# A spectral block and a gMLP on one core: Gelus, a third product's w, and w_in's later tiles put at other chunks

## The chip, the core and the metric

The kernel runs on one core of a Trainium2 chip. The metric is the device time of one execution in microseconds, and the time of a kernel is the median of its runs. The core's engines run side by side: TensorE (PE) multiplies matrices, VectorE (DVE) and ScalarE (ACT) work elementwise, GpSimd (POOL) and SyncE (SP) mostly issue transfers here. Each takes its instructions strictly in the order of the program.

## The reference

Two sublayers stand one after the other, both modulated by a condition `c`:

```python
h = layernorm(x) * (1 + ca) + sa
x = x + ga * (Cr @ (h @ Hr.T) - Ci @ (h @ Hi.T))      # 2048 x 2048 and 512 x 512 DFT matrices
h = layernorm(x) * (1 + cb) + sb
z = gelu(h @ w_in)                                    # 512 -> 1792
z1, z2 = z[..., :896], layernorm(z[..., 896:])
x = x + gb * ((z1 * (w_sp @ z2 + b_sp)) @ w_out)      # w_sp 2048 x 2048, w_out 896 -> 512
```

`x` is 2048 x 512, all in fp32. sa, ca, ga, sb, cb, gb are six rows of `silu(c) @ w_mod`.

## The kernel before, in words

Every fp32 operand is split into a rounded part and a rest (`ah` and `al` for the streamed side, `wh`/`wl`, `w`, `wih`/`wil` and others for the weights), and each product is three matmuls: rounded by rounded, rounded by rest, rest by rounded (`matmul3`, lines 95 to 97). ACT writes the rounded part (line 249 for `ah`), DVE the rest (line 256 for `al`).

The program is one long list of chunks n. Up to N2 they are the DFT over the sequence, from N2 to N3 the first half of `z` (z1), from N3 to N4 the second half (z2), after N4 the product with `w_sp`, and last `w_out`. The order on each engine is written out by hand: `at(n, f, ...)` puts a piece of work at chunk n, and `run(n)` issues what was put there, ahead of the chunk's matmuls in the z1 stage; `prep(n)` ahead of that issues `al` for chunk n + 2 and `ah` for chunk n + 3.

The change lies in the z1 stage. It computes z1 for the four row blocks in two pairs (q = 0, 1), each by seven products (a Strassen-like scheme, `FORMS = (1, 2, 6, 7, 4, 5, 3)`) of two chunks each. So c = n - N2 counts 0 to 27, the first pair is c = 0 to 13, the second c = 14 to 27. Chunks of products 1, 2, 6 and 4 have four column tiles f (12 matmuls), those of 7, 5 and 3 have three (9 matmuls). In the first pair c = 6, 7 is product 7, c = 8, 9 product 4, c = 10, 11 product 5, c = 12, 13 product 3; in the second pair 14 later. Several products add up in the same PSUM banks, so between them somebody has to read a sum out before TensorE goes on:

- After product 7, ACT copies the three banks of `z1g` to `z1k` (line 669); product 4 then goes on in these banks.
- After product 5, DVE adds `z1k` to the three banks of `z1p` (line 677); product 3 then goes on in them. ACT applies the Gelu to the sum later (line 679).
- After products 2 and 4, `gelu_z1` (lines 682 to 686) applies the Gelu to four banks (line 685), each into a tile `z` of the pool tag `z1row`, and POOL stores each tile to DRAM (`z_d`, line 686). That tag has seven buffers, used in turn. For product 2 of the first pair the Gelus were put three chunks after the product, that is at c = 6.

```python
z = zrow[0].tile([P, Q], F32, tag="z1row", bufs=NF, name=f"z1_{q}_{p}_{f}")
nc.scalar.activation(z, acc[f], AF.Gelu_apprx_tanh)
nc.gpsimd.dma_start(z1_d[2 * q + (p == 4)][f], z)
```

Around that stand other pieces: `hi_w(3)` and `lo_w(3)` split the weights of product 3 (line 641 on ACT, line 644 on DVE); `turn_z` transposes blocks of h on DVE (line 597); `load` (line 154) and `load_wi` (line 565) issue loads on SP, `stage<-h_d` being blocks of h; `make_wi` (line 575, ACT) and `make_wi_lo` (line 578, DVE) split the four tiles of w_in's second half (`wih`, `wil`) for the z2 stage; `sum_s` (lines 728 to 739) forms sums of blocks of `w_sp` on DVE and stores them by POOL. The tags `wil2` and `wil3` are also the buffers of product 7's weights.

Of the kernel before, what the change touches and what calls it, by code (L numbers as in the profile page):

```python
# [9 lines left out]
F32R = mybir.dt.float32r  # L10
# [3 lines left out]
P = 128  # L14
# [5 lines left out]
def fnet_gmlp_kernel(  # L20
# [35 lines left out]
    FH = F2 // 2  # L56
# [22 lines left out]
    def bank(k, name):  # L79
        return psum.tile([P, 512], F32, tag=f"bank{k}", bufs=1, name=name)  # L80
# [12 lines left out]
    def matmul3(acc, ah, al, bh, bl, first, last, go_on=False):  # L93

        nc.tensor.matmul(acc, ah, bh, start=first, stop=False, skip_group_check=go_on)  # L95
        nc.tensor.matmul(acc, ah, bl, start=False, stop=False, skip_group_check=go_on)  # L96
        nc.tensor.matmul(acc, al, bh, start=False, stop=last, skip_group_check=go_on)  # L97
# [25 lines left out]
    def at(n, f, *a):  # L123
        fill.setdefault(n, []).append((f, a))

    def run(n):
        for f, a in fill.pop(n, []):
            f(*a)
# [55 lines left out]
    def prep(n):  # L184

        if n not in prepared:
            prepared.add(n)
            if later_hi(n + 2):
                prep_hi(n + 2)
            prep_lo(n + 2)  # L190
            if n % 2 == 0 and n and not N2 + 4 <= n + 4 < N3:
                turn_two(n + 4)
            if n and not later_hi(n + 3):
                prep_hi(n + 3)
# [362 lines left out]
    wi_hi, wi_lo, wraw, ZT = {}, {}, {}, {}  # L557
# [12 lines left out]
    def make_wi(e, k):  # L570
        if k == 0:
            wi_hi[e] = wpool[0].tile([P, ND, FH], F32R, tag="wih", bufs=1, name="wih1")
        wi_hi[e, k] = wi_hi[e][:, k, :]
        wi_lo[e, k] = wpool[0].tile([P, FH], F32R, tag=f"wil{k}", bufs=1, name=f"wil{e}_{k}")
        nc.scalar.activation(wi_hi[e, k], wraw[e, k], AF.Copy)

    def make_wi_lo(e, k):
        nc.vector.tensor_tensor(wi_lo[e, k], wraw.pop((e, k)), wi_hi[e, k].bitcast(F32), op=ALU.subtract)

    WR, WF, ZG = {}, {}, {}  # L580
# [65 lines left out]
    def mm_z1(n):  # L646
        q, c = divmod(n - N2, NP)
        p, k = FORMS[c // 2], c % 2
        nf = 4 if p in (1, 2, 6, 4) else 3
        here, there = (0, 4) if q == 0 else (4, 0)  # L650
        if k == 0 and p in (1, 5):
            for f in range(nf):
                ZT[f] = bank(here + f, f"z1p{q}_{p}_{f}")
        acc = ZG if p in (6, 7, 4) else ZT
        th, tl = AH.pop(n), AL.pop(n)
        for f in range(nf):
            w, cols = WF[1 if f == 3 else p] if p == 6 else WF[p], slice(f * P, (f + 1) * P)
            matmul3(acc[f], w[0][:, k, cols], w[1][:, k, cols], th, tl,
                    k == 0 and p in (1, 5), k == 1, p not in (1, 5))
        if k == 0:  # L660
            return
        if p == 1:
            for f in range(4):
                ZG[f] = bank(there + f, f"z1g{q}_{f}")
                nc.scalar.activation(ZG[f], ZT[f], AF.Copy)
        elif p in (6, 7):
            for f in range(3):
                G[p, f] = bpool[0].tile([P, Q], F32, tag="bh" if p == 6 else "bl", bufs=3, name=f"z1k{q}_{p}_{f}")
                nc.scalar.activation(G[p, f], ZG[f], AF.Copy)
        elif (q, p) == (0, 2):  # L670
            at(n + 3, gelu_z1, q, p, dict(acc))
        elif p in (2, 4):
            gelu_z1(q, p, acc)
        else:
            m = 7 if p == 5 else 6
            for f in range(3):
                nc.vector.tensor_tensor(G[m, f], ZT[f], G[m, f], op=ALU.add)
            for f in range(3):
                nc.scalar.activation(G[m, f], G[m, f], AF.Gelu_apprx_tanh)
                nc.gpsimd.dma_start(z1_d[2 * q + (p == 5)][4 + f], G.pop((m, f)))  # L680

    def gelu_z1(q, p, acc):
        for f in range(4):
# [3 lines that stand above are left out]
# [261 lines left out]
    for s, n in ((4, 4), (5, 4), (6, 6), (7, 6), (8, 10), (9, 10)):  # L948
        m = n + (s == 9)
# [23 lines left out]
    for j, turn, weigh, row, fold, hi in ((0, (25, 26, 27, 28), (29, 29, 30, 30), 26, (34, 34, 35, 36), (38, 35, 36, 37)),  # L973
# [8 lines left out]
        n = weigh[3] + (3 if j == 0 else 1)  # L982
# [13 lines left out]
    for t in range(NQ):  # L996
        n = 8 * NQ * (t + 1)
# [35 lines left out]
    wpool, zpool, zrow, bpool, spre, gpool = [], [], [], [], [], []  # L1033
# [12 lines left out]
    at(84, change_q)  # L1046
    for i, u in enumerate((r, g, b) for g in range(2) for b in range(4) for r in range(2)):
        n = 85 + 5 * i if i < 8 else N2 + (13, 15, 28, 29, 31, 33, 35, 37)[i - 8]
        m = n + (4 if i < 8 or i > 9 else (8, 11)[i - 8])
        at(n, load_s, *u)  # L1050
        at(m, sum_s, *u, True)
        at(m + 1, sum_s, *u, False)
# [7 lines left out]
    for c, *todo in ((2, (norm_y, 3, 2), (hi_w, 6), (lo_w, 6), (sum_w, 7)),  # L1060
                     (3, (norm_y, 3, 3), (sum_w, 4), (post_h, 3, 2), (hi_w, 7), (lo_w, 7)),
                     (4, (hi_w, 4), (lo_w, 4), (post_h, 3, 3), (change_s,), (load, N2 // 4 + 3)),
                     (6, (sum_z4, 0), (hi_w, 5), (lo_w, 5)), (8, (turn_z, 2), (hi_w, 3)), (9, (lo_w, 3), (load_wi, 1, 0)),
                     (10, (load_wi, 1, 2)), (12, (turn_z, 3)), (14, (sum_z, 1)),
                     (17, (make_wi, 1, 0), (make_wi_lo, 1, 0)), (18, (make_wi, 1, 1), (make_wi_lo, 1, 1)),
                     (19, (sum_z4, 1)), (22, (make_wi, 1, 2), (make_wi_lo, 1, 2)), (24, (make_wi, 1, 3), (make_wi_lo, 1, 3))):
        for f, *a in todo:
            at(N2 + c, f, *a)
    for n in range(N2, N3):
        prep(n)  # L1070
        run(n)
        mm_z1(n)

    zstack = ctx.enter_context(ExitStack())

# [5 lines left out]
    for i, p in enumerate(PROD):  # L1081
        for k in range(8):
            n = NB[p] + 2 * k
# [39 lines left out]
    for f in range(NF):  # L1123
        n = NB[6] + 3 * f
# [66 lines left out]
```

## Time and profile before

| | |
|---|---|
| median of 3 runs | 949.35 us (948.96 to 949.91) |
| profiled execution, its own time | 948.98 us |
| its span, first to last instruction | 947.2 us |
| TensorE busy | 940.0 us (99%) |
| VectorE / ScalarE / GpSimd busy | 704.0 / 388.4 / 174.3 us |
| granted clock of TensorE | 1.0 in every slice |

A busy time is the union of an engine's instructions. In a timeline, "0.33 <-ACT z1k" behind an instruction says that its engine stood idle 0.33 us before it, and what ended that. A matmul's shown length (0.39 us) is longer than the step to the next one, since matmuls overlap.

### The profile page before, as it was taken

The numbers are of one execution on the slowest core, as the hardware profiler recorded it, in microseconds if no ns is written. First come the engines' busy times: TensorE is split into PE (matmuls) and PEld (weight loads), VectorE is DVE, ScalarE is ACT, GpSimd is POOL, SyncE is SP. The second block draws the span as 40 slices with busy tenths as digits, with TensorE's granted clock in tenths as the row PEclk, the third lists the DMA queues.
The fourth block names the chain that finished last, engine by engine and source line by source line (L and its number), as shares of the span: only waits on it lengthen the run. The fifth ranks groups of instructions, "written<-read, shape, count | busy, mean of one in ns | idle before, by whom it ended". The sixth has DMA issues, their size and how long they took to land.

```text
span 947.2 us, 12274 instructions
## 1 busy us (share of the span) xinstructions
PE 940.0 (99%) x4160; PEld 781.3 (82%) x4160; DVE 704.0 (74%) x1039; ACT 388.4 (41%) x665; POOL 174.3 (18%) x331
## 2 busy tenths in 40 slices
PE   8999999999999999999999999999999999999998
PEld 5888888888888888888888999888888888888886
DVE  6799857775576667767978588877788688885872
ACT  4685424232132222322776356644544444331221
POOL 2430000221531144122332265200000000000000
PEclk9999999999999999999999999999999999999999
DMA  9996553576437975996397985555554456833541
GB/s 213 222 222 149 113 139 89 147 187 156 134 89 195 274 212 153 279 280 140 126 307 281 327 266 152 155 114 134 128 133 90 105 118 140 206 102 120 192 162 57
DMA packets 249230, 161.25 MB, mean 170 GB/s; under 512 B 130192, under 2 KB 218512, under 8 KB 249040
## 3 DMA queue, kind: packets, MB, share of 16 engines
q1 hardware_dynamic: 235792, 120.75, 52.8%
q0 software_dynamic: 11984, 39.07, 11.3%
q10 hardware_dynamic: 1392, 0.66, 0.3%
q8 instruction: 32, 0.52, 0.2%
q14 instruction: 30, 0.25, 0.1%
HBM read 123.73 MB, written 36.70 MB: 169 GB/s over the span
## 4 chain that ended last, share of the span: by engine, by line
PE 95%; DMA 2%; DVE 1%; ACT 1%; POOL 1%; issue 0%; ACTq 0%; SPq 0%; POOLq 0%; DVEq 0%
PE gp L95 12%; PE gp L96 12%; PE gp L97 12%; PE gw L96 10%; PE gw L97 10%; PE gw L95 10%; PE yp L96 3%; PE yp L95 3%; PE yp L97 3%; PE z2p L97 3%; PE z2p L96 3%; PE z2p L95 3%; PE op L96 3%; PE op L95 3%; PE op L97 3%; PE z1p L95 1%
## 5 line engine op out<-in xcount | busy, mean ns | idle before, releaser
L249 ACT ACTIVATE ah<-t 128x512 fp32r<-128x512 f32 x263 | 164.2, 627 | 306.6 <-PE gp L97 184.9
L256 DVE TENSOR_TENSOR al<-t,ah 128x512 fp32r<-128x512 f32 x264 | 180.1, 685 | 142.7 <-PE gp L96 65.3
L95 PE MATMUL gp<-ah,hh 128*128 128x512 f32 x496 | 192.9, 389 | 0.0
L96 PE MATMUL gp<-al,hh 128*128 128x512 f32 x496 | 192.9, 389 | 0.0
L97 PE MATMUL gp<-ah,hl 128*128 128x512 f32 x496 | 192.9, 389 | 0.0
L97 PE MATMUL gw<-ah,bl 128*128 128x512 f32 x400 | 155.6, 389 | 0.0
L96 PE MATMUL gw<-al,bh 128*128 128x512 f32 x400 | 155.6, 389 | 0.0
L95 PE MATMUL gw<-ah,bh 128*128 128x512 f32 x400 | 155.6, 389 | 0.0
L97 PEld LDWEIGHTS gp<-ah,hl 128*128 128x128 f32 x496 | 93.1, 188 | 19.4
L95 PEld LDWEIGHTS gp<-ah,hh 128*128 128x128 f32 x496 | 93.1, 188 | 19.3
L96 PEld LDWEIGHTS gp<-al,hh 128*128 128x128 f32 x496 | 93.1, 188 | 19.2
L95 PEld LDWEIGHTS gw<-ah,bh 128*128 128x128 f32 x400 | 75.1, 188 | 15.7
L97 PEld LDWEIGHTS gw<-ah,bl 128*128 128x128 f32 x400 | 75.1, 188 | 15.5
L96 PEld LDWEIGHTS gw<-al,bh 128*128 128x128 f32 x400 | 75.1, 188 | 15.5
L220 DVE STREAM_TRANSPOSE t<-stage 128x1024 f32<-128x1024 f32 x64 | 79.2, 1238 | 5.8 <-DMA stage<-in_A_dft_seq_re_dram 5.4
L214 DVE STREAM_TRANSPOSE t<-stage 128x1024 f32<-128x1024 f32 x56 | 69.3, 1238 | 0.0
L761 ACT ACTIVATE bh<-z 128x512 fp32r<-128x512 f32 (+1 forms) x56 | 32.8, 587 | 65.8 <-PE gw L96 65.8
L739 POOL DMA_DIRECT2D s_d<-sj x64 | 35.1, 550 | 110.5 <-DVE sj L731 81.5
L95 PE MATMUL yp<-hth,gh 128*128 128x512 f32 x128 | 49.8, 389 | 0.0
L96 PE MATMUL yp<-htl,gh 128*128 128x512 f32 x128 | 49.8, 389 | 0.0
L97 PE MATMUL yp<-hth,gl 128*128 128x512 f32 x128 | 49.8, 389 | 0.0
L96 PE MATMUL z2p<-wil,ah 128*128 128x448 f32 x128 | 46.7, 365 | 0.0
(204 smaller groups left out, 1419.3 us busy)
## 6 DMA issues: line engine op xcount, KB each, us to landing
stage<-in_A_dft_seq_im_dram SPq DMA_DIRECT2D x64, 256.0 KB, 5.5
sj<-in_B_w_sp_dram SPq DMA_DIRECT2D x32, 512.0 KB, 8.3
s_d<-sj POOLq DMA_DIRECT2D x64, 256.0 KB, 4.3
stage<-s_d SPq DMA_DIRECT2D x128, 128.0 KB, 2.9
stage<-in_A_dft_seq_re_dram SPq DMA_DIRECT2D x60, 256.0 KB, 5.3
stage<-in_B_w_sp_dram SPq DMA_DIRECT2D x96, 128.0 KB, 3.2
stage<-h_d SPq DMA_DIRECT2D x32, 256.0 KB, 6.0
wm<-in_w_mod_dram SPq DMA_DIRECT2D x16, 256.0 KB, 4.8
```

Source lines behind the costliest of these rows:

```text
L95: nc.tensor.matmul(acc, ah, bh, start=first, stop=False, skip_group_check=go_on)
L96: nc.tensor.matmul(acc, ah, bl, start=False, stop=False, skip_group_check=go_on)
L97: nc.tensor.matmul(acc, al, bh, start=False, stop=last, skip_group_check=go_on)
L214: nc.vector.transpose(t.rearrange("p r (b i) -> p r b i", i=32), st[:, :, :, 16 * k:16 * k + 32])
L220: nc.vector.transpose(t.rearrange("p k (b i) -> p k b i", i=32), st[:, :, 32 * k:32 * k + 64].rearrange("p b (k i) -> p k b i", k=2))
L249: nc.scalar.activation(AH[n], source(n), AF.Copy)
L256: nc.vector.tensor_tensor(AL[n], source(n), AH[n].bitcast(F32), op=ALU.subtract)
L739: nc.gpsimd.dma_start(s_d[m, r, g][b * P:(b + 1) * P, :], a)
L761: nc.scalar.activation(BH[p, k][:, :w], b_of(p, k), AF.Copy)
```

## The change

The Gelus of product 2 in the first pair are put five chunks after the product in place of three (c = 8 in place of 6). `hi_w(3)` goes from c = 8 and `lo_w(3)` from c = 9 to c = 10. The ACT parts of w_in's third and fourth tile go from c = 22 to 20 and from c = 24 to 22; the DVE part of the third goes from c = 22 to 21.5, which is run behind the matmuls of c = 21, and that of the fourth stays at 24. The tile `wil` is now taken in `make_wi_lo` and no longer in `make_wi`. The sums of one `w_sp` block (i = 8) go from c = 21 and 22 to c = 22 and 23.

```diff
@@ -571,10 +571,10 @@
         wi_hi[e, k] = wi_hi[e][:, k, :]
+        nc.scalar.activation(wi_hi[e, k], wraw[e, k], AF.Copy)
+
+    def make_wi_lo(e, k):
         wi_lo[e, k] = wpool[0].tile([P, FH], F32R, tag=f"wil{k}", bufs=1, name=f"wil{e}_{k}")
-        nc.scalar.activation(wi_hi[e, k], wraw[e, k], AF.Copy)
-
-    def make_wi_lo(e, k):
         nc.vector.tensor_tensor(wi_lo[e, k], wraw.pop((e, k)), wi_hi[e, k].bitcast(F32), op=ALU.subtract)
@@ -668,7 +668,7 @@
         elif (q, p) == (0, 2):
-            at(n + 3, gelu_z1, q, p, dict(acc))
+            at(n + 5, gelu_z1, q, p, dict(acc))
@@ -1046,7 +1046,7 @@
-        m = n + (4 if i < 8 or i > 9 else (8, 11)[i - 8])
+        m = n + (4 if i < 8 or i > 9 else (9, 11)[i - 8])
@@ -1060,16 +1060,18 @@
-                     (6, (sum_z4, 0), (hi_w, 5), (lo_w, 5)), (8, (turn_z, 2), (hi_w, 3)), (9, (lo_w, 3), (load_wi, 1, 0)),
-                     (10, (load_wi, 1, 2)), (12, (turn_z, 3)), (14, (sum_z, 1)),
+                     (6, (sum_z4, 0), (hi_w, 5), (lo_w, 5)), (8, (turn_z, 2)), (9, (load_wi, 1, 0)),
+                     (10, (hi_w, 3), (lo_w, 3), (load_wi, 1, 2)), (12, (turn_z, 3)), (14, (sum_z, 1)),
-                     (19, (sum_z4, 1)), (22, (make_wi, 1, 2), (make_wi_lo, 1, 2)), (24, (make_wi, 1, 3), (make_wi_lo, 1, 3))):
+                     (19, (sum_z4, 1)), (20, (make_wi, 1, 2)), (21.5, (make_wi_lo, 1, 2)), (22, (make_wi, 1, 3)),
+                     (24, (make_wi_lo, 1, 3))):
     for n in range(N2, N3):
         prep(n)
         run(n)
         mm_z1(n)
+        run(n + 0.5)
```

How this moves the instructions, at three places. First ACT in the first pair, before, from product 5's weights to the copies of product 7 (`w_4178` is product 5's rounded w, `z_0_2_*` product 2's Gelus, `ah_4205` the rounded part for c = 10):

```order
L641 ACTIVATE w_4178<-wraw_0_3923 128x768
L685 ACTIVATE z_0_2_0_4182<-z1p_1_0_4020 128x512
L685 ACTIVATE z_0_2_1_4185<-z1p_1_1_4021 128x512
L685 ACTIVATE z_0_2_2_4188<-z1p_1_2_4022 128x512
L685 ACTIVATE z_0_2_3_4191<-z1p_1_3_4023 128x512
L249 ACTIVATE ah_4205<-hs_3979 128x512 [waits DVE_49,PE_49,Activation_49]
L669 ACTIVATE z1k_7_0_4216<-z1g_0_4048 128x512 [waits DVE_49,PE_49]
L669 ACTIVATE z1k_7_1_4218<-z1g_1_4050 128x512 [waits PE_49]
L669 ACTIVATE z1k_7_2_4220<-z1g_2_4052 128x512 [waits PE_49]
```

And ACT now, from behind product 7's copies (which directly follow `w_4178` and the `ah` for c = 10) to product 3's weights (`z_0_4_*` are product 4's Gelus, `w_4283` product 3's rounded w):

```order
L249 ACTIVATE ah_4212<-hs_3979 128x512 [waits DVE_49,Activation_49]
L685 ACTIVATE z_0_2_0_4222<-z1p_1_0_4020 128x512
L685 ACTIVATE z_0_2_1_4225<-z1p_1_1_4021 128x512
L685 ACTIVATE z_0_2_2_4228<-z1p_1_2_4022 128x512
L685 ACTIVATE z_0_2_3_4231<-z1p_1_3_4023 128x512
L249 ACTIVATE ah_4248<-t_3762 128x512 [waits DVE_49,PE_49,Activation_49]
L685 ACTIVATE z_0_4_0_4267<-z1g_0_4048 128x512 [waits PE_49]
L685 ACTIVATE z_0_4_1_4270<-z1g_1_4050 128x512 [waits PE_49]
L685 ACTIVATE z_0_4_2_4273<-z1g_2_4052 128x512 [waits PE_49]
L685 ACTIVATE z_0_4_3_4276<-z1g_3_4054 128x512 [waits DMASW4_49,PE_49,Activation_49]
L249 ACTIVATE ah_4281<-t_3762 128x512 [waits DVE_49]
L641 ACTIVATE w_4283<-wraw_2_3928 128x768
```

Product 2's Gelus now stand behind the copies and directly ahead of product 4's; product 3's w stood ahead of product 4's Gelus and stands behind them. The wait on DMASW4 in `z_0_4_3` is for the store of `z_0_2_0`, whose buffer it takes, the eighth tile of seven buffers. It stood there before too.

Second, DVE in the first pair, where `w_4284` (`w_4235` before) is the rest of product 3's w, `al_4304` that for c = 13, and line 677 the sums in product 5's banks:

```order
-L644 TENSOR_TENSOR w_4235<-wraw_2_3928,w_4234 128x768 [waits Activation_49]
-L256 TENSOR_TENSOR al_4283<-t_3762,ah_4251 128x512 [waits DVE_49,PE_49,Activation_49]
-L256 TENSOR_TENSOR al_4304<-t_3762,ah_4285 128x512 [waits DVE_49,PE_49,Activation_49]
-L677 TENSOR_TENSOR z1k_7_0_4216<-z1p_5_0_4292,z1k_7_0_4216 128x512 [waits PE_49]
```

```order
+L256 TENSOR_TENSOR al_4279<-t_3762,ah_4248 128x512 [waits DVE_49,PE_49,Activation_49]
+L644 TENSOR_TENSOR w_4284<-wraw_2_3928,w_4283 128x768 [waits Activation_49]
+L256 TENSOR_TENSOR al_4304<-t_3762,ah_4281 128x512 [waits DVE_49,PE_49]
+L677 TENSOR_TENSOR z1k_7_0_4204<-z1p_5_0_4292,z1k_7_0_4204 128x512 [waits PE_49]
```

The rest of w went from two places ahead of `al_4304` to one, so it is the last but one ahead of the sums of line 677.

Third, DVE in the second pair now (`wil_2` and `wil_3` are the rests of w_in's third and fourth tile, `sj` the w_sp block's sums, `al_4622` the rest for c = 27):

```order
L578 TENSOR_TENSOR wil_2_4546<-wraw_2_4287,wih_4443 128x896
L256 TENSOR_TENSOR al_4548<-hs_4376,ah_4529 128x512
L731 TENSOR_TENSOR sj_4351<-sj_4351 128x512
L732 TENSOR_TENSOR sj_4351<-sj_4351 128x512
L256 TENSOR_TENSOR al_4569<-hs_4376,ah_4550 128x512
L735 TENSOR_TENSOR sj_4351<-sj_4351 128x512
L736 TENSOR_TENSOR sj_4351<-sj_4351 128x512
L256 TENSOR_TENSOR al_4601<-hz_4214,ah_4571 128x512
L217 STREAM_TRANSPOSE t_4603<-stage_4217 128x4x4x32 x2
L578 TENSOR_TENSOR wil_3_4608<-wraw_2_4287,wih_4443 128x896
L256 TENSOR_TENSOR al_4622<-hz_4214,ah_4606 128x512
L677 TENSOR_TENSOR z1k_7_0_4540<-z1p_5_0_4610,z1k_7_0_4540 128x512
```

`wil_2` stood behind the four sums of `sj` and stands ahead of them, each of the two pairs of sums with one `al` more ahead of it; `wil_3` keeps its place, but its ACT half now comes two chunks earlier.

## Rows read from the trace of the kernel before

**Rows 1.** The page, busy time, share and count by engine.
```profile
PE 940.0 (99%) x4160; PEld 781.3 (82%) x4160; DVE 704.0 (74%) x1039; ACT 388.4 (41%) x665; POOL 174.3 (18%) x331
```
**Rows 2.** Waits of PE, whole run, without the start's: total us, times, longest.
```profile
...
PE z1p L95 <- DVE z1k L677: 0.4, 1, 0.4
...
PE z1g L95 <- ACT z1k L669: 0.3, 1, 0.3
```
**Rows 3.** Timeline of PE, start us and us, first pair (c = 8, c = 12).
```profile
468.41 0.39 PE L97 MATMUL z1g<-ah,w 128*128 128x512 f32 x1
469.13 0.50 PE L95 MATMUL z1g<-ah,wh 128*128 128x512 f32 x1 [0.33 <-ACT z1k L669]
469.46 0.40 PE L96 MATMUL z1g<-al,wh 128*128 128x512 f32 x1
...
478.78 0.39 PE L95 MATMUL z1p<-ah,w 128*128 128x512 f32 x1
```
**Rows 4.** Timeline of PE, second pair, the start of c = 26.
```profile
512.55 0.39 PE L97 MATMUL z1p<-ah,w 128*128 128x512 f32 x1
513.33 0.47 PE L95 MATMUL z1p<-ah,w 128*128 128x512 f32 x1 [0.39 <-DVE z1k L677]
```
**Rows 5.** Timeline of ACT, first pair.
```profile
465.30 0.83 ACT L641 ACTIVATE w<-wraw 128x768 fp32r<-128x768 f32 x1
466.03 2.04 ACT L685 ACTIVATE z<-z1p 128x512 f32<-128x512 f32 x4
467.94 0.65 ACT L249 ACTIVATE ah<-hs 128x512 fp32r<-128x512 f32 x1
468.46 1.59 ACT L669 ACTIVATE z1k<-z1g 128x512 f32<-128x512 f32 x3
...
472.86 2.69 ACT L685 ACTIVATE z<-z1g 128x512 f32<-128x512 f32 x4
```
**Rows 6.** Timeline of ACT, second pair, copies of product 7.
```profile
501.47 0.63 ACT L249 ACTIVATE ah<-hs 128x512 fp32r<-128x512 f32 x1 [1.46 <-PE z1g L97]
502.10 1.96 ACT L669 ACTIVATE z1k<-z1g 128x512 f32<-128x512 f32 x3
```
**Rows 7.** Timeline of DVE, first pair.
```profile
468.14 0.95 DVE L644 TENSOR_TENSOR w<-wraw,w 128x768 fp32r<-128x768 f32 x1
469.01 0.68 DVE L256 TENSOR_TENSOR al<-hz,ah 128x512 fp32r<-128x512 f32 x1
469.61 0.68 DVE L256 TENSOR_TENSOR al<-hs,ah 128x512 fp32r<-128x512 f32 x1
...
477.62 2.05 DVE L677 TENSOR_TENSOR z1k<-z1p,z1k 128x512 f32<-128x512 f32 x3 [0.16 <-PE z1p L97]
```
**Rows 8.** Timeline of DVE, second pair.
```profile
503.83 0.69 DVE L731 TENSOR_TENSOR sj<-sj 128x512 f32<-128x512 f32 x1 [1.89 <-DMA sj<-in_B_w_sp_dram]
...
508.74 0.69 DVE L256 TENSOR_TENSOR al<-hz,ah 128x512 fp32r<-128x512 f32 x1
...
510.89 1.10 DVE L578 TENSOR_TENSOR wil<-wraw,wih 128x896 fp32r<-128x896 f32 x1 [0.24 <-ACT wih L575]
...
512.50 1.88 DVE L677 TENSOR_TENSOR z1k<-z1p,z1k 128x512 f32<-128x512 f32 x3
```
**Rows 9.** Timelines of SP and of POOL, first pair: issues of transfers.
```profile
468.64 6.93 SPq L154 DMA_DIRECT2D stage<-h_d  x8
...
473.75 0.54 POOL L686 DMA_DIRECT2D z_d<-z  x1 [4.71 <-ACT z L685]
```
**Rows 10.** DMA issues of four stretches (466.9, 468.5, 473.75, 475.84 us): us to landing.
```profile
z_d<-z POOLq DMA_DIRECT2D x1, 256.0 KB, 2.4
...
z_d<-z POOLq DMA_DIRECT2D x1, 256.0 KB, 4.6
...
z_d<-z POOLq DMA_DIRECT2D x1, 256.0 KB, 6.0
...
z_d<-z POOLq DMA_DIRECT2D x1, 256.0 KB, 6.8
```

More of the change, by code (lines that the diff above doesn't have):

```diff
@@ L573, in make_wi @@
         wi_hi[e, k] = wi_hi[e][:, k, :]
-        wi_lo[e, k] = wpool[0].tile([P, FH], F32R, tag=f"wil{k}", bufs=1, name=f"wil{e}_{k}")
         nc.scalar.activation(wi_hi[e, k], wraw[e, k], AF.Copy)
     def make_wi_lo(e, k):
+        wi_lo[e, k] = wpool[0].tile([P, FH], F32R, tag=f"wil{k}", bufs=1, name=f"wil{e}_{k}")
         nc.vector.tensor_tensor(wi_lo[e, k], wraw.pop((e, k)), wi_hi[e, k].bitcast(F32), op=ALU.subtract)
```

## The prediction

> **What bounds the kernel now.** I read the page first: TensorE is busy for 940.0 of 947.2 us [rows 1]. So a change of order can only give back TensorE's idle time, or add to it. Next came TensorE's waits over the whole run. Behind the program's start, which the change doesn't touch, there are just two, both in the z1 stage [rows 2]. The timeline of TensorE prices them. Undisturbed, matmuls start 0.227 us apart: from 469.46 to 478.78 there are 41 steps [rows 3]. At c = 8 the step is 0.72 and the next one 0.33 in place of 0.23, which makes 0.60 us lost to the copies of product 7 [rows 3]. At c = 26 the step is 0.78; with the same slow second step 0.65 us are lost, to the sums of line 677 [rows 4]. Both together are 1.25 us, 0.13% of the time. What a measurement of this kernel can tell from no change is about 0.2%, 1.9 us. So the change can't be measurably faster; the question is whether it makes a new wait.
>
> **The Gelus of product 2, c = 6 to 8.** Before, ACT runs w, the four Gelus (2.04 us), `ah` and only then the copies, which start at 468.46 [rows 5], though the first bank is complete when its last matmul is, before 467.5 (its tile is the first of three in c = 7, whose last matmul starts at 468.41 [rows 3]). In the second pair, where no Gelus stand ahead, `ah` and copies run directly after each other from 501.47 [rows 6], and TensorE has no wait there [rows 2]. So the first wait goes: **-0.60 us**, and TensorE would start c = 12 at 478.78 - 0.60 = 478.18.
>
> The Gelus themselves, 2.0 us, move into a stretch of ACT that was half idle, and nobody on TensorE waits for them before c = 10. But what hangs on their stores does wait. The buffer of the first Gelu tile is taken again by the last Gelu of product 4 once the store has landed. Before, this store is issued at 466.90 with nothing else under way and lands in 2.4 us [rows 10], long before the last Gelu of product 4 (its four end at 475.55 [rows 5]). Now: the last copy starts after the last matmul of c = 7 (468.41 + 0.39, and 0.1), takes 0.65 (1.96 for three [rows 6]) and ends at 469.5; `ah` follows, and 0.52 later [rows 5], at 469.9, the first Gelu. A store is issued 0.89 us after its Gelu starts (472.86 and 473.75 [rows 5, 9]): at 470.8. By then SP has been issuing eight loads of 256 KB since 468.64 [rows 9]; these wait for the stores of h, not for any Gelu, so they don't move. A store that meets these loads lands after 4.6 us (issued at 468.5, as they begin) to 6.8 (475.84, at their end); one issued in their midst at 473.75 needs 6.0 [rows 10]. Lower bound 2.4, the lone store, upper bound 6.8. I take 5.3, midway between 4.6 and 6.0, since at 470.8 about half of the loads are ahead of it. It then lands at 476.1, and the last Gelu of product 4, which could have run to 475.55 - 0.60 = 474.95, runs from 476.2 to about 476.8 (0.6 each, four in 2.04 to 2.69 [rows 5]).
>
> **Product 3's w, c = 8 and 9 to 10.** It stands behind that Gelu now. Counted from the Gelu's end E: `ah` starts at E - 0.13 and w 0.52 later (466.03 + 2.04 against 467.94, then 468.46 [rows 5]); w takes 0.83 [rows 5]; the rest of w on DVE 0.87 and an `al` 0.60 to the next start [rows 7]; then the first sum of line 677, and 0.83 after its start TensorE (512.50 and 513.33 [rows 8, 4]). That is E + 3.5 with some hundredths between engines, call it 3.55. Before, these sums waited for TensorE alone: 0.16 idle at 477.62 [rows 7]. With E = 474.95, were there no store, TensorE would start c = 12 at 478.50 instead of 478.18, 0.42 lost with the slow second step. With E = 476.8 it starts at 480.35: 2.17 and 0.1, **+2.27 us**. The load of w_in's second half waits for the rest of w on SP, and so issues later; it is first read at c = 20, ten chunks on (some 23 us at 9 to 12 steps each), and costs nothing.
>
> **w_in's third and fourth tile, and the sums a chunk later.** ACT's part at c = 20 fits into the 1.46 us for which ACT was idle ahead of 501.47 [rows 6]. `wil_2` writes a buffer of product 7's weights, so it can't start before c = 21 ends. That is 42 matmuls before 512.78 (512.55 + 0.23 [rows 4]), at 503.2, just when DVE sat idle for 1.89 us until 503.83 [rows 8]. From 503.4 it takes 1.1, the four sums 0.7 each, two `al` 0.6 each: done by 508.5, still ahead of the `al` at 508.74 that follows TensorE [rows 8]. `wil_3` no longer waits 0.24 us for ACT [rows 8], and the sums of line 677, two instructions behind it, start that much earlier: **-0.24 us** of the second wait. Nothing on this path depends on the first pair's delay, since both follow TensorE. The stores of the sums go a chunk later through POOL, ahead of the Gelus' stores as before; nothing reads them before the `w_sp` stage, cost 0.
>
> **Sum:** -0.60 + 2.27 - 0.24 = +1.43 us on the profiled 948.98, 950.4. The median of the runs lies 0.37 higher, 949.35, so I forecast **950.8 us**, +0.15%, too little to be told from no change. With the landing at 4.6 to 5.8 us it is 950.1 to 951.3.
>
> **Rivals.**
> 1. *The store lands later*, the side of slower. Place: the last Gelu of product 4. Each us of landing time is a us on TensorE; from 5.8 us on the whole passes +1.9. At the 6.8 us of the last store in the stretch the sum is 1.43 + 1.5 = 2.93: 952.3. For it: all stores later in the stretch took 6.0 and more [rows 10]. Against: those had SP's next loads (w_in) around them, and more loads ahead.
> 2. *The store is not in the way*: it lands within 3.4 us of its issue. Then -0.60 + 0.42 - 0.24 = -0.42: 948.9. For it: a lone store takes 2.4, and this one is not issued last. Against: the store at 468.5, with only the first loads near it, took 4.6 already [rows 10]. The Trainium skill, "DMA: Bandwidth & Descriptors", section "Queues, rings and completion order", says that each DMA engine takes turns between the queues that have work, packet by packet; by that the store would share with one load at a time and not stand behind several. The trace speaks against it, with 6.0 us for 256 KB at 473.75 as against 2.4 alone.
> 3. *Both old waits go altogether and none comes*: -1.25, 948.1. It needs the rest of w to be done before the sums' banks are complete, which the chain above denies by 0.3 us.
> 4. *w_in's move does nothing*: if `wil_2` pushes the `al` at 508.74 back by more than the 0.24 us won, the second wait stays: 951.0, inside the forecast's range.
>
> **How the numbers follow.** Forecast with rival 4: 0.61. Rival 1: 0.23. Rival 2: 0.13. Rival 3: 0.03. Faster by over 0.2% would need more than all idle time there is: 0.02 for what I don't see. Slower by over 0.2%: 0.24, nearly all rival 1. Same: 0.74. The forecast's own range is 950.1 to 951.3; to hold 8 in 10 it must reach to 952.3, rival 1's time, and down to 949.0, which takes in some of rival 2 with the scatter of the runs (0.4 us below the median).
>
> **What would show it.** In the changed profile TensorE's wait for the copies at c = 8 is gone, and c = 8 starts at about 468.6. The store of the first Gelu is issued near 470.8 and lands near 476; ACT stands idle, released by that store, ahead of the last Gelu of product 4; TensorE waits about 2.2 us for line 677 at c = 12; at c = 26 its wait shrinks from 0.39 to about 0.15. I am wrong if ACT has no idle time ahead of that Gelu (rival 2), if the store takes over 5.8 us (rival 1), if the copies still hold c = 8, or if the granted clock drops from 1.0 behind the wait, which no row here shows for a pause of that length.

## The result, and the profile after

| | before | after |
|---|---|---|
| median | 949.11 us (948.80 to 949.91, 18 runs) | 950.51 us (949.72 to 952.68, 18 runs) |
| profiled execution, its span | 948.98, 947.2 us | 952.28, 950.5 us |
| mean granted clock of the profiled execution | 1.0 | 0.998 |

The ratio is 1.0018, with a 95% interval of 1.001 to 1.0025; by the medians the change costs 1.40 us, 0.15%. That is less than the 0.2% that the prediction took for the least that can be told from no change, but the interval lies above 1: 18 runs against 18 do tell it. The forecast was 950.8 us, in a range of 949.0 to 952.3, and the working made the difference +1.43 us. Of the 18 runs, 14 lie between 949.72 and 950.71 (median 950.45) and four between 952.18 and 952.68, all four at a mean granted clock of 0.998. The profiled execution is one of these four; what they have in addition is the last part of this section.

TensorE is still the bound [rows 1]. Its count of matmuls is the same; the 1.8 us that it is busy longer come of the slower matmuls shown below:

```profile
PE 941.8 (99%) x4160; PEld 782.7 (82%) x4160; DVE 703.7 (74%) x1039; ACT 388.5 (41%) x665; POOL 174.5 (18%) x331
```

In TensorE's waits the row of the copies [rows 2] is gone, and that of line 677 is five times as long (and belongs to another place, c = 12 and no longer c = 26):

```profile
PE z1p L95 <- DVE z1k L677: 2.2, 1, 2.2
```

TensorE's timeline says where. The last column in brackets is the idle time before an instruction and what ended it.

```profile
468.65 0.39 PE L97 MATMUL z1g<-ah,w 128*128 128x512 f32 x1
468.87 0.39 PE L95 MATMUL z1g<-ah,wh 128*128 128x512 f32 x1
...
474.09 0.39 PE L97 MATMUL z1g<-ah,wl 128*128 128x512 f32 x1
...
478.17 0.39 PE L97 MATMUL z1p<-ah,w 128*128 128x512 f32 x1
480.73 0.47 PE L95 MATMUL z1p<-ah,w 128*128 128x512 f32 x1 [2.17 <-DVE z1k L677]
481.03 0.40 PE L96 MATMUL z1p<-al,w 128*128 128x512 f32 x1
...
481.73 0.62 PE L96 MATMUL z1p<-al,w 128*128 128x512 f32 x1
...
485.14 0.40 PE L95 MATMUL z1p<-ah,w 128*128 128x512 f32 x1
...
516.23 0.39 PE L97 MATMUL z1p<-ah,w 128*128 128x512 f32 x1
516.65 0.47 PE L95 MATMUL z1p<-ah,w 128*128 128x512 f32 x1
```

At c = 8 the step from 468.65 to 468.87 is the undisturbed one: the wait for the copies [rows 3] is gone. At c = 12 the step is 2.56 us, and the next 0.30: 2.41 us are lost. At c = 26 the step is 0.42 us where it was 0.78 [rows 4].

ACT shows what c = 12 hangs on: product 2's Gelus and three of product 4's, then 2.10 us of nothing, then the fourth, and behind it `ah` and product 3's w.

```profile
470.09 2.05 ACT L685 ACTIVATE z<-z1p 128x512 f32<-128x512 f32 x4
472.00 0.66 ACT L249 ACTIVATE ah<-t 128x512 fp32r<-128x512 f32 x1
472.52 1.92 ACT L685 ACTIVATE z<-z1g 128x512 f32<-128x512 f32 x3
476.54 0.60 ACT L685 ACTIVATE z<-z1g 128x512 f32<-128x512 f32 x1 [2.10 <-PE z1p L97]
477.03 0.62 ACT L249 ACTIVATE ah<-t 128x512 fp32r<-128x512 f32 x1
477.55 0.83 ACT L641 ACTIVATE w<-wraw 128x768 fp32r<-128x768 f32 x1
```

The page puts the idle time down to TensorE. But TensorE's last matmul into these banks, at the end of c = 9, started at 474.09 and was done by 474.5, two microseconds earlier, so it is another of the semaphores that the Gelu waits for. The DMA issues (SP's first four loads of h, issued from 468.87 to 470.29, and then POOL's first store of z, issued at 470.97) name it; the last number is the us to landing:

```profile
stage<-h_d SPq DMA_DIRECT2D x1, 256.0 KB, 3.0
...
stage<-h_d SPq DMA_DIRECT2D x1, 256.0 KB, 3.8
...
stage<-h_d SPq DMA_DIRECT2D x1, 256.0 KB, 5.4
...
stage<-h_d SPq DMA_DIRECT2D x1, 256.0 KB, 5.5
...
z_d<-z POOLq DMA_DIRECT2D x1, 256.0 KB, 5.5
```

The four loads land at 471.9, 473.1, 475.1 and 475.8, the store at 476.4, and the Gelu starts at 476.54. What the two queues moved in between is in the trace's view of DMA, from 471.0 to 474.2 us (packets, MB, time of the packets as a share of 16 engines):

```profile
q1 hardware_dynamic: 1387, 0.69, 110.5%
q0 software_dynamic: 4, 0.02, 2.4%
```

q1 is SP's queue and q0 POOL's (where SP issues nothing, as in one run below, only q0 moves). The store was issued at 470.97, and its data did not begin to move before 474.1, when SP's four loads were nearly through.

On DVE the rest of w follows, an `al` and the sums, and 0.84 us after the first sum's start TensorE goes on. The last three rows are the second pair's, with w_in's fourth rest and the sums for c = 26:

```profile
478.42 0.96 DVE L644 TENSOR_TENSOR w<-wraw,w 128x768 fp32r<-128x768 f32 x1 [3.38 <-ACT w L641]
479.29 0.69 DVE L256 TENSOR_TENSOR al<-t,ah 128x512 fp32r<-128x512 f32 x1
479.89 1.28 DVE L677 TENSOR_TENSOR z1k<-z1p,z1k 128x512 f32<-128x512 f32 x2
...
513.03 1.30 DVE L217 STREAM_TRANSPOSE t<-stage 128x512 f32<-128x512 f32 x2
514.25 1.05 DVE L578 TENSOR_TENSOR wil<-wraw,wih 128x896 fp32r<-128x896 f32 x1
...
515.82 1.88 DVE L677 TENSOR_TENSOR z1k<-z1p,z1k 128x512 f32<-128x512 f32 x3
```

What was not in the sum is in the rows behind the wait: eight matmuls, from 481.73 to 485.14, stand 0.43 us apart in place of 0.227 and take 0.63 us in place of 0.39. Busy time by stretch, with the granted clock in the last column but two:

```profile
476.00:478.00 2.00, 2.00 (x11) 1.65 (x10) 0.00 (x0) 1.46 (x3) 0.54 (x1) 1.00 1.09 392
478.00:481.00 3.00, 0.83 (x4) 0.43 (x3) 2.58 (x4) 1.29 (x3) 0.00 (x0) 1.00 1.04 365
481.00:482.00 1.00, 1.00 (x5) 0.83 (x4) 1.00 (x3) 1.00 (x3) 0.46 (x1) 0.86 1.23 283
482.00:485.00 3.00, 3.00 (x8) 2.32 (x8) 3.00 (x4) 1.59 (x3) 1.16 (x3) 0.50 1.10 300
485.00:488.00 3.00, 3.00 (x14) 2.40 (x14) 2.88 (x6) 1.81 (x4) 0.85 (x2) 0.98 1.02 271
```

From 482 to 485 the clock stands at 0.50, that is 1.2 GHz in place of 2.4. It costs 3.41 - 8 x 0.227 = 1.6 us. TensorE had been busy without a gap up to the wait, stood still for 2.2 us and ran again for a microsecond before the clock fell. The ledger of this execution: +0.23 from the program's first 10 us, -0.60 at c = 8, +2.41 at c = 12, +1.6 for the clock, -0.36 at c = 26: +3.28, against 952.28 - 948.98 = 3.30.

### The profile page after: what moved, and what is told of

Read it like the earlier page. It is cut to its first block, busy times and chain, and to the rows that moved or that the text cites. A ratio compares the mean times of both kernels' runs of the same rounds, so it can differ in the third digit from the quotient of the medians.

```text
span 950.5 us, 12276 instructions
## 1 busy us (share of the span) xinstructions
PE 941.8 (99%) x4160; PEld 782.7 (82%) x4160; DVE 703.7 (74%) x1039; ACT 388.5 (41%) x665; POOL 174.5 (18%) x331
## 5 line engine op out<-in xcount | busy, mean ns | idle before, releaser
L95 PE MATMUL z2p<-wih,ah 128*128 128x448 f32 x128 | 46.8, 365 | 0.0
```

## The experiments

Four theories stood against each other. **S**: the store of the first Gelu lands late behind SP's loads, and the last Gelu of product 4 waits for its buffer. **A**: ACT is simply too full there. **W**: it is product 3's w that comes too late at its new place. **C**: the half clock comes of TensorE standing still.

The diffs are cut to what changes. Each ratio is to the kernel before, run beside it (medians 949.10 to 949.19), with its 95% interval.

**Take the buffer away.** The last Gelu of product 4 gets a tile of its own and no longer waits for any store; nothing else moves.

```diff
-            z = zrow[0].tile([P, Q], F32, tag="z1row", bufs=NF, ...)
+            if (q, p, f) == (0, 4, 3):
+                z = zpool[-1].tile([P, FH], F32, tag="zb7", bufs=1, ...)[:, :Q]
+            else:
+                z = zrow[0].tile([P, Q], F32, tag="z1row", bufs=NF, ...)
```

> The changed kernel, but the last Gelu tile of product 4 in the first pair takes a buffer of its own (one of the z2 stage's, free until then), so that nothing waits for the store of product 2's first Gelu. Theory S (that store, behind the four loads of h, holds the last Gelu, and with it product 3's w and the sums of line 677): TensorE's wait at c = 12 falls from 2.2 to about 0.3 us, no idle time of ACT ahead of that Gelu, time about 1.8 to 2.0 below the changed kernel's 950.51, at 948.6. Theory A (ACT has simply too much to do between c = 8 and c = 11, store or not): the wait stays near 2.2 and the time at 950.5.

Measured: 948.47 us (948.30 to 948.93), ratio 0.9994 (0.9985 to 1.0002). ACT's four Gelus run through, and TensorE's row is down to a tenth:

```profile
PE z1p L95 <- DVE z1k L677: 0.2, 1, 0.2
...
472.67 2.59 ACT L688 ACTIVATE z<-z1g 128x512 f32<-128x512 f32 x4
```

S holds and A falls: ACT has the same work in the same order and no lateness, and the slowest of the 11 runs is below the fastest of the changed kernel (949.72). The 0.2 us left are w's chain, which the working had put at 0.42 lost (0.39 here, the slow second step with it).

**Store earlier.** Only the first of product 2's Gelus goes back to c = 6, so that its store is issued at 467.13, before SP's loads.

```diff
-            at(n + 5, gelu_z1, q, p, dict(acc))
+            at(n + 3, gelu_z1, q, p, dict(acc), range(1))
+            at(n + 5, gelu_z1, q, p, dict(acc), range(1, 4))
```

> The changed kernel, but the first of product 2's four Gelus in the first pair stays at c = 6, so that its store is issued some 3.5 us earlier, ahead of the loads of h; the other three stay at c = 8. Theory S: the store lands in 2.4 to 3 us as in the kernel before, the last Gelu of product 4 doesn't wait, c = 12 waits about 0.3; ACT had 0.72 us idle ahead of the ah for c = 10, which takes the one Gelu, so the copies stay early and c = 8 waits not at all or under 0.1; 948.6. Theory A: the work of ACT between c = 8 and 11 is 0.5 us less, so the wait at c = 12 is still about 1.7, 950.0.

Measured: 948.60 us (948.34 to 949.40), ratio 0.9994 (0.9984 to 1.0003). The store lands in 2.3 us, ACT doesn't wait, TensorE waits 0.2 us at c = 12 and not at c = 8. The same work at another time on the queue is worth as much as the extra buffer.

**Each part by itself.** On the kernel before: only the Gelus to c = 8; only the move in w_in with the sums; only product 3's w to c = 10. All three intervals include 1, so what each part does is read from the steps of one trace each, and the medians only agree with it.

```diff
-            at(n + 3, gelu_z1, q, p, dict(acc))
+            at(n + 5, gelu_z1, q, p, dict(acc))
```

> The kernel before with one part of the change alone: product 2's Gelus at c = 8. Theory S: the first store is issued at about 471.7 (w stands ahead of the Gelus now) and lands near 477, the last Gelu of product 4 ends near 477.2; w is no longer behind it, but the al for c = 13 and the sums of line 677 are, so c = 12 starts at E + 1.9 in place of E + 3.55: a wait of 0.6 to 1.3, 0 to 0.8 us lost on the whole: 949.2 to 949.9. Theory W (product 3's w at c = 10 is needed for the wait): no wait at c = 12, 948.5.

Measured: 949.03 us (948.74 to 949.48), ratio 0.9999 (0.999 to 1.0008), somewhat below what was expected. The store, issued at 471.71, landed after 4.3 us where 5.3 was expected. The Gelu waits for it here too, and in this execution the row names the store itself:

```profile
476.14 0.60 ACT L685 ACTIVATE z<-z1g 128x512 f32<-128x512 f32 x1 [1.28 <-DMA z_d<-z]
```

With w already done ahead of the Gelu, the late store costs TensorE 0.41 us (steps of 0.56 and 0.31), little enough to be paid for by the 0.60 won at c = 8. The move of w_in, by itself (with its `run(n + 0.5)` and the place of the tile `wil`):

```diff
-(22, (make_wi, 1, 2), (make_wi_lo, 1, 2)), (24, (make_wi, 1, 3), (make_wi_lo, 1, 3))
+(20, (make_wi, 1, 2)), (21.5, (make_wi_lo, 1, 2)), (22, (make_wi, 1, 3)), (24, (make_wi_lo, 1, 3))
-        m = n + (4 if i < 8 or i > 9 else (8, 11)[i - 8])
+        m = n + (4 if i < 8 or i > 9 else (9, 11)[i - 8])
```

> The kernel before with the second pair's part of the change alone: w_in's third and fourth tile and the w_sp sums a chunk later. All theories: the wait at c = 8 stays (0.60 us), no wait at c = 12, that at c = 26 falls from 0.63 to 0.27: 948.8. If the part did nothing: 949.1.

Measured: 948.81 us (948.58 to 949.33), ratio 0.9997 (0.9988 to 1.0006); the step at c = 8 stays at 0.72, that at c = 26 falls from 0.78 to 0.42. And w:

```diff
-(8, (turn_z, 2), (hi_w, 3)), (9, (lo_w, 3), (load_wi, 1, 0)), (10, (load_wi, 1, 2))
+(8, (turn_z, 2)), (9, (load_wi, 1, 0)), (10, (hi_w, 3), (lo_w, 3), (load_wi, 1, 2))
```

> The kernel before with one part of the change alone: product 3's w at c = 10. Theory S: the store lands early, so the chain from the last Gelu of product 4 (its end at 475.55, plus 3.55) reaches c = 12 about 0.3 late: wait of 0.3 at c = 12, 0.4 us lost, the old waits at c = 8 and c = 26 as before: 949.5. Theory W (the place of product 3's w is the cause whatever the Gelus do): a wait near 2 us at c = 12, 951.3.

Measured: 949.60 us (949.38 to 949.92), ratio 1.0004 (0.9996 to 1.0013). TensorE loses 0.44 us at c = 12 and the other two waits stay. So W falls as the whole cause: w alone costs 0.44, the late store alone 0.41, and both in a row on ACT 2.41, since w then starts only when the late Gelu is done.

**A buffer less.** Six in place of seven, so that two Gelus wait for the stores.

```diff
-tag="z1row", bufs=NF,
+tag="z1row", bufs=NF - 1,
```

> The changed kernel with six buffers for the Gelu tiles in place of seven: the last Gelu of product 4 then takes the buffer of product 2's second tile, whose store landed 0.61 us after the first one's. Theory S: the wait at c = 12 grows by about 0.6 us, to 2.8, and the median to 951.1; the granted clock falls behind it at least as often as in the changed kernel. Theory A: nothing changes, 950.5.

Measured: 952.68 us (951.62 to 954.28, 5 runs), ratio 1.0037 (1.0024 to 1.0049). The last two Gelus come late, as expected, but the size was missed: the wait of TensorE grew by 0.1 us only, since in this execution the stores of both buffers landed in 5.0 us. What raised the median is the clock: four of the five runs show 0.996 to 0.998.

```profile
475.85 1.13 ACT L685 ACTIVATE z<-z1g 128x512 f32<-128x512 f32 x2 [2.35 <-DMA z_d<-z]
...
480.57 0.60 PE L95 MATMUL z1p<-ah,w 128*128 128x512 f32 x1 [2.27 <-DVE z1k L677]
480.97 0.63 PE L96 MATMUL z1p<-al,w 128*128 128x512 f32 x1
```

**Fill the wait.** The same, with nine matmuls into a free bank ahead of c = 12, which nothing reads.

```diff
+        if n == N2 + 12:
+            ps = bank(3, "busyz")
+            for _ in range(9):
+                nc.tensor.matmul(ps, AH[n][:, :P], AH[n], start=True, stop=True)
```

> The kernel with six buffers (median 952.68, granted clock 0.998 or lower in four of five runs), with nine added matmuls of 512 columns ahead of c = 12 that write a free bank and are read by nobody. They need 2.04 us, less than the wait of 2.3 us. Theory C (the half clock behind the wait comes from TensorE's standing still): the first true matmul of c = 12 starts when it did, the clock stays 1.0 in every run, and the 1.6 us that eight matmuls at double step cost are gone: about 951.0, no run over 952. Rival: the clock falls for another reason, and the runs stay at 952 to 954.

Measured: 951.33 us (950.74 to 952.67, 8 runs), ratio 1.0024 (1.0014 to 1.0034), the clock at 0.999 or 1.0 in each run. The nine fill most of the wait, and the matmuls behind it come at the full rate:

```profile
479.69 2.20 PE L1076 MATMUL busyz<-ah 128*128 128x512 f32 x9
482.72 0.47 PE L95 MATMUL z1p<-ah,w 128*128 128x512 f32 x1 [0.84 <-DVE z1k L677]
483.03 0.40 PE L96 MATMUL z1p<-al,w 128*128 128x512 f32 x1
```

With TensorE busy through most of the wait, the lateness costs no clock, though it is larger here (3.26 us from the last true matmul of c = 11 to the first of c = 12, against 2.66 with six buffers), and the median is 1.35 us lower. Two expectations were missed: c = 12 still waits 0.84 us, since the stores took 5.5 and 5.6 us in place of 5.0, and one run, the profiled one, is over 952 (952.67). That one had lost 1.4 us at 319 us of the program, where TensorE waited 1.2 us for DVE in another stage. Eight of eight at full against one of five speaks for C. It is not proof: the two kernels ran on different chips, and on the second chip no kernel was run with the wait left empty.

**Which loads hold up the store?** On the kernel after, four of h's loads go to POOL, behind the stores (the expectation says eight; the other four found a free buffer and were issued by SP at 437.0, long before this stage).

```diff
-(4, (hi_w, 4), (lo_w, 4), (post_h, 3, 3), (change_s,), (load, N2 // 4 + 3)),
+(4, (hi_w, 4), (lo_w, 4), (post_h, 3, 3), (change_s,)),
...
-(9, (load_wi, 1, 0))
+(9, (load_pool, N2 // 4 + 3), (load_wi, 1, 0))
```

> The changed kernel, but the first eight loads of h (block t = 3) are issued by POOL at c = 9, behind the stores of product 2's Gelus, and not by SP at c = 4 (where they ran from 468.9 on). Nothing else moves. Theory S (the store of the first Gelu is slow since it stands behind SP's loads): the store, issued at about 471.0, lands in some 2.5 us, long before the last Gelu of product 4 wants its buffer; no wait of ACT there, the wait of TensorE at c = 12 falls from 2.2 to about 0.2 to 0.3, clock 1.0 behind it, time 948.6. Rival R (the store is slow at that place for another reason, such as four stores in a row on POOL's queue, whatever SP does): it still takes 5 us or more, the wait stays at about 2.2 and the time at 950.5. A third way: the loads of h, now later, make a new wait of DVE's transposes in the second pair; that would show as a wait on stage, not on z_d.

Measured: 950.78 us (950.47 to 952.44), ratio 1.002 (1.0011 to 1.0029). A miss, and one that told nothing yet: SP, with h's loads gone, went on to its next four (w_in's second half), issued from 469.24 to 470.54. The first and the last of them, and the store, issued at 470.86:

```profile
wraw<-in_B_w_in_dram SPq DMA_DIRECT2D x1, 224.0 KB, 3.1
...
wraw<-in_B_w_in_dram SPq DMA_DIRECT2D x1, 224.0 KB, 5.7
...
z_d<-z POOLq DMA_DIRECT2D x1, 256.0 KB, 5.2
```

So these four go to POOL as well, and SP has nothing to issue:

```diff
-(load_wi, 1, 0)
+(load_wi, 1, 0, nc.gpsimd)
```

> As the run with h's loads on POOL, where SP simply went on to its next four loads (w_in's second half, 224 KB each, issued at 469.24 to 470.54) and the store of the first Gelu, issued at 470.86, still landed behind them, after 5.2 us: there only the name of the loads had changed, and the theories were not told apart. Here these four go to POOL too, behind the stores and h's loads, so that SP issues nothing from 469 until the rest of product 3's w is done. Theory S (SP's loads hold the store up): the store lands in 2.3 to 3 us, no wait of ACT for it, the wait at c = 12 falls to 0.2 or 0.3, time 948.6 to 948.9. Rival R (the store is slow for itself, or through its three followers on POOL's own queue): it still takes 5 us, the wait stays near 2 us and the time at 950.5.

Measured: 948.74 us (948.46 to 949.23), ratio 0.9997 (0.9988 to 1.0006). The store, issued at 470.71 with the same three stores behind it, and what follows from it:

```profile
z_d<-z POOLq DMA_DIRECT2D x1, 256.0 KB, 2.3
...
472.25 2.65 ACT L689 ACTIVATE z<-z1g 128x512 f32<-128x512 f32 x4
...
PE z1p L95 <- DVE z1k L681: 0.2, 1, 0.2
```

With no load of SP ahead of it the same store at the same place takes 2.3 us in place of 5.2 to 5.5. S holds to its root: the four loads ahead of it on SP's queue, whatever they carry. Whether they would hold it up as much from POOL's own queue was not run.

**A better order.** The own buffer, w back at c = 8 and 9, and w_in's fourth rest out of the way of c = 26. In a first try it went behind, to c = 26 itself:

```diff
-(24, (make_wi_lo, 1, 3))
+(26, (make_wi_lo, 1, 3))
```

> The changed kernel with the last Gelu tile of product 4 in a buffer of its own, product 3's w back at c = 8 and 9, and the DVE half of w_in's fourth tile at c = 26, behind the sums of line 677, in place of 24. Theory S: none of the waits at c = 8, 12 and 26 is left; the 1.25 us of both old waits are gone: 947.9, against 949.1 of the kernel before. Theory A: with w ahead of the Gelus ACT is fuller still ahead of c = 12, a wait of 0.5 or more there, 948.4 or more.

Measured: 948.76 us (948.27 to 949.98), ratio 0.9998 (0.9989 to 1.0007). The three waits were gone, but DVE did that rest (1.08 us) right ahead of an `al` of z2, and TensorE waited there:

```profile
517.88 0.47 PE L97 MATMUL z2p<-wih,al 128*128 128x448 f32 x1 [0.41 <-DVE al L256]
```

In the profiled execution (949.98, one of three of the 11 runs near 949.95) all of z2's matmuls then came 0.206 us apart, where they come 0.199 to 0.207 apart elsewhere; why is not known. The second try puts it ahead, at c = 23:

```diff
-(24, (make_wi_lo, 1, 3))
+(23, (make_wi_lo, 1, 3))
```

> The changed kernel with the own buffer for product 4's last Gelu, product 3's w back at c = 8 and 9, and w_in's fourth rest at c = 23, one chunk ahead of where the change has it. If the three waits are just a matter of the order in this stage, c = 8, c = 12 and c = 26 all start without a wait, which is 1.25 us below the kernel before: 947.9. Moving the fourth rest to c = 23 and not c = 26 leaves the start of the z2 stage as it was, so the wait there for al of the run with c = 26 should be absent. If the second stage's matmuls come 0.206 us apart in place of 0.200 again (some 380 of them), the gain is given back: about 949.2.

Measured: 947.81 us (947.64 to 948.57), ratio 0.9987 (0.9978 to 0.9995): 1.3 us below the kernel before, which its interval tells from no change, and 2.7 below the change. The places of c = 8, c = 12, c = 26 and of z2's start:

```profile
468.65 0.39 PE L97 MATMUL z1g<-ah,w 128*128 128x512 f32 x1
468.88 0.39 PE L95 MATMUL z1g<-ah,wh 128*128 128x512 f32 x1
...
478.17 0.39 PE L97 MATMUL z1p<-ah,w 128*128 128x512 f32 x1
478.40 0.39 PE L95 MATMUL z1p<-ah,w 128*128 128x512 f32 x1
...
512.17 0.39 PE L97 MATMUL z1p<-ah,w 128*128 128x512 f32 x1
512.40 0.39 PE L95 MATMUL z1p<-ah,w 128*128 128x512 f32 x1
...
516.25 0.39 PE L97 MATMUL z1p<-ah,w 128*128 128x512 f32 x1
516.48 0.36 PE L95 MATMUL z2p<-wih,ah 128*128 128x448 f32 x1
```

From 468.88 to 516.48 not one step is longer than the others. It is all that this stage had to give: the 1.25 us of the two old waits.

## Why the prediction was right

- **The wait at c = 8** went, as worked out: -0.60. It is also gone with the Gelus moved alone.
- **The landing of the store.** Taken as 5.3 us, chosen between 4.6 and 6.0 because about half of SP's eight loads would be ahead of it. It was 5.5, and four were ahead. That it came so near is in part luck: in the five traces with four loads ahead of the same store it took 5.0 to 5.5. The three stores behind it took as long or longer, but land in order behind the same loads. The runs on the loads show that they are the cause.
- **The chain behind the Gelu.** From the Gelu's end to TensorE it was put at 3.55 us. The last Gelu ended at 477.14 and TensorE went on at 480.73: 3.59. The loss at c = 12 came to 2.41 against +2.27; of the difference 0.11 is the Gelu's later end, which is the landing's, and 0.04 the chain. A sum by rows of single instructions held to 0.05 us over six instructions on three engines.
- **Product 3's w.** Without the late store it was to lose 0.42 at c = 12; the run with the own buffer lost 0.39, w by itself 0.44.
- **c = 26**: -0.36 against -0.24. The sums start 0.41 us ahead of TensorE's last matmul (515.82, 516.23), where it was 0.05 [rows 4, 8]. What was left out: the idle 0.24 us count from the end of the transposes ahead, but with nothing to wait for the rest starts 0.08 us before their end (513.03 + 1.30 against 514.25). Sign and place were right, the size a tenth of a microsecond short.
- **The sum.** +1.43 was forecast, the three terms measured make -0.60 + 2.41 - 0.36 = +1.45, the medians +1.40. So close an agreement is luck: 0.14 more was lost at c = 12 and 0.12 more won at c = 26, and the two cancel. The forecast of 950.8 was 0.3 high because it added 0.37 us for a median of three runs; over 18 runs the kernel before is at 949.11, 0.13 above its profiled execution.
- **What a measurement can tell** was put at 0.2%. With 18 runs each, 0.15% is told from no change, and so is the gain of the best version, 0.13%, with 11.
- **w_in's load and the sums' stores** were costed at nothing, and no new wait shows.
- **The clock** was named as what would make the working wrong, with no row to price it. It fell in four of 18 runs, for 1.6 us by the rows and 1.9 by the medians (952.35 of the four against 950.45 of the 14). The median lies among the 14 that it did not touch, so the forecast was met without this cost; had the clock fallen in most runs, as with six buffers, the time would have been near 952.3. Rival 1's time of 952.3 was met by these four runs, for a reason that is not rival 1's.
- **The rivals.** Rival 2 would have had no idle time on ACT. The Trainium skill, "DMA: Bandwidth & Descriptors", section "Queues, rings and completion order", says that each DMA engine takes turns between queues, packet by packet. The trace does not bear that out: from 471.0 to 474.2 us SP's queue moved 1387 packets and POOL's four, with the store waiting. It landed after 5.0 to 5.5 us with four of SP's loads just ahead of it, against 2.3 without them. Why the queues took no turns stays open. Rival 3's 948.1 needed another order, and the best version has it (947.81). Rival 4 is refuted by the run with w_in's move alone.

## What to carry to other kernels

When an edit moves work on one engine, ask when the transfers that hang on it will now be issued and what stands in the DMA queues at that moment: here moving 2 us of Gelus won 0.60 us, and a store that left 4 us later for it, just behind four loads, cost 2.41. A ring of buffers that is long enough for stores of 2.4 us can be one too short for 5.5; one more buffer, or an issue ahead of the loads, is worth as much. And when loads are moved out of the way, see what the queue issues in their place.

## What was not expected of the hardware

- A wait of 2.2 us of TensorE, in the midst of full work, let the granted clock fall to half for some 3.4 us, but only in some runs: four of 18, three of 11 with h's loads moved (952.12 to 952.44), and four of five with six buffers. It costs 1.6 us, beside 2.4 for the wait. With nine added matmuls in the wait it stayed at full in eight runs of eight, on another chip. Behind the waits of 0.3 to 0.8 us in this stage it stayed at full in every trace.
- A store on POOL's queue waited for SP's loads ahead of it nearly as if all stood in one line: landings at 471.9, 473.1, 475.1, 475.8 (loads) and 476.4 (store), with only four of POOL's packets moved from 471.0 to 474.2 us. It is not a strict order of issue: with w_in's loads ahead, the store landed at 476.1 and the last of them at 476.2.
- The distance of z2's matmuls of 448 columns varies between 0.199 and 0.207 us, and in one execution all were at 0.206 to 0.207. What sets it stayed open.
